# Output products of a Sinkhorn-attention and max-out kernel by Strassen's algorithm, with its sums on three engines and its steps in one list

## The chip, the cores and the metric

One Trainium2 chip, one of its cores. The core has TensorE (PE, with its weight loads shown apart as PEld), VectorE (DVE), ScalarE (ACT), GpSimd (POOL) and SyncE (SP), which run side by side and wait for each other through semaphores; transfers run on 16 DMA engines, fed by SP's queue and POOL's queue. The metric is the device time of one execution in microseconds (us), lower is better. Before: 166.56 us, the median of 3 runs (165.94 to 166.78).

## The reference

There are 4 batches, 8 heads, 768 positions and 64 elements a head. A Sinkhorn-normalised 8x8 matrix per batch and head mixes the 8 blocks (96 positions each) of keys and of values; each block of queries then attends to its own mixed block. The result, 768 tokens of 512 for each batch, goes through a max-out layer.

```python
for _ in range(5):
    P = P - np.max(P, axis=-1, keepdims=True)
    P = np.exp(P)
    P = P / (np.sum(P, axis=-1, keepdims=True) + 1e-09)
    P = P / (np.sum(P, axis=-2, keepdims=True) + 1e-09)
k_sorted = np.einsum('bhij,bhjcd->bhicd', P, k_b).reshape(B, H, S, D)
v_sorted = np.einsum('bhij,bhjcd->bhicd', P, v_b).reshape(B, H, S, D)
...
scores = scale * np.matmul(q_b, k_sb.transpose(0, 1, 2, 4, 3))
...
x = np.ascontiguousarray(attn_out.transpose(0, 2, 1, 3)).reshape(B * S, H * D)
h1 = x @ w1
h2 = x @ w2
g = np.maximum(h1, h2)
return (g @ w_out).astype(np.float32)
```

w1 and w2 are 512x1024, w_out is 1024x512, x has 3072 rows.

## The kernel before, in words

The max-out is rewritten: max(h1, h2) = relu(x(w1 - w2)) + x w2, so the output is relu(x(w1 - w2)) w_out + x (w2 w_out). The kernel forms w1 - w2 once (`w_difference`, two quarters of it on POOL), transposes w2 on TensorE and forms w2 w_out once into `wc` (`w_product`, line 657). The output of a batch is then one product with 12 blocks of 128 in its inner dimension: 8 blocks of g (`g_tiles`) against `wo_sb` and 4 blocks of x transposed (`xT`) against `wc`. All matmul operands are bf16, sums are fp32.

A batch passes these steps, each of which takes one PSUM tile (two banks; there are four such tiles) and frees it when an engine has read it: `sort_k` (line 458, three per batch) mixes the keys; `sort_v`, `sort_v_pair`, `sort_v_halved` (lines 479, 523, 500) mix the values, from `v_dc`, a turned copy of `v_raw` made in column quarters by `turn_v` (line 250); `q_transposes` (lines 433 and 419) turn the queries, on TensorE in batches 0 and 1 and by a DMA transpose on SP's queue in batches 2 and 3, from `q_pair`, which `pair_q` (line 407) copies together; `scores` (line 548; exp on ACT, line 556, into one of NE buffers e); `values` (line 575; reciprocal and multiplication on DVE, lines 586 and 592); `x_transposes` (line 605), a DMA transpose on SP's queue from batch 1 on, four per batch; `moe_h` (line 677; relu on ACT or DVE), eight per batch, one for each half of the batch's tokens (`ch`) and two 128-blocks of g; and `moe_out` (line 704), which for a tile of 128 tokens runs 12 matmuls of 512 columns. Two tiles share a PSUM tile, which ACT or DVE copies out whole (1024 columns) and SP stores (512 KB). The last two token tiles of batch 3 are done by `moe_out_last` (lines 737 to 740), in one piece of 512 columns and two of 384 and 128, the last one copied and stored by ACT.

xT of one batch has halves by `ch` and, within each, two parts that come from one `x_transposes` each: the parts 0 and 1 belong to ch 0, the parts 2 and 3 to ch 1. A `moe_h` of ch 1 reads part 2 in its first two matmuls and part 3 in the next two.

Loads of k, q, v and weights are issued by POOL (lines 143, 160, 169, 182, 189). Batch 3's keys and queries are loaded into `v_raw`, once `turn_v` has emptied it: `load_k(3)` into its first half of columns, `load_q(3)` into the second.

The order on each engine is the order of the program's text (manual schedule). After a hand-written front for batch 0, four loops over `units` (line 848 on) run the h and output units of a batch, and tables (`first_tail`, `second_tail`, `third_tail`) say which attention steps of the next batch follow which unit. `pick` gives each PSUM read to ACT or DVE by running loads.

Of the kernel before, what the change touches and what calls it, by code (L numbers as in the profile page):

```python
# [10 lines left out]
FP32 = mybir.dt.float32  # L11
BF16 = mybir.dt.bfloat16
# [4 lines left out]
def kernel(  # L17
# [24 lines left out]
    G = B * H  # L42
# [10 lines left out]
    NE = 8  # L53
# [188 lines left out]
    def turn_v(rows, eng, c0, c1):  # L242
# [6 lines left out]
        else:  # L249
            nc.vector.tensor_copy(  # L250
# [152 lines left out]
    def pair_q(b, two):  # L403

        if two == 0:
            q_pair[b] = qpool.tile([128, HP, R, 2 * D], BF16, tag="q_pair", name="q_pair", bufs=1)
        nc.vector.tensor_copy(
            out=q_pair[b][:, :, :, two * D : (two + 1) * D],
            in_=q_raw[b][:, two * HP : (two + 1) * HP].rearrange("p h (r d) -> p h r d", r=R),
        )  # L410
        load["D"] += 900
# [125 lines left out]
    e_tiles, x_tiles = {}, {}  # L537

    def scores(b, u, n=0):
# [15 lines left out]
        e = e_bufs[(b * 8 + u) % NE]  # L555
# [98 lines left out]
    def w_product(dmt):  # L654
        ps = ps_f32("wc_ps")
        for fb in range(NFB):
            nc.tensor.matmul(  # L657
                ps[:, 0:512],
                w2T[:, fb, dmt * 128 : (dmt + 1) * 128],
                wo_sb[:, fb, :],  # L660
                start=(fb == 0),
                stop=(fb == NFB - 1),
            )
        evac(wc[:, dmt, :], ps[:, 0:512], 512)
# [33 lines left out]
    out_ps = {}  # L698

    def out_products(dst, b, ti, n0=0, n1=512, part=None):  # L700
        ch, off = divmod(ti * 128, TCH)
        for m in range(NFB + HP) if part is None else range(part * 6, part * 6 + 6):
            hp = m - NFB
            nc.tensor.matmul(  # L704
                dst,
                g_tiles[b, ch, m // 2][:, m % 2, off : off + 128]
                if m < NFB
                else xT[:, b % 2, ch, hp % 2, hp // 2, off : off + 128],
                wo_sb[:, m, n0:n1] if m < NFB else wc[:, hp, n0:n1],
                start=(m == 0),  # L710
                stop=(m == NFB + HP - 1),
            )

    def moe_out(b, ti, part):
        slot = ti % 2
        if slot == 0 and part == 0:
            out_ps[0] = ps_f32("out_ps")
        ps = out_ps[0]
        out_products(ps[:, slot * 512 : (slot + 1) * 512], b, ti, part=part)
        if slot == 1 and part == 1:  # L720
            tok0 = b * S + ti * 128
            o = opool.tile([128, 2, 512], FP32, tag="o", name="o")
            evac(o.rearrange("p t n -> p (t n)"), ps, 1024)
            nc.sync.dma_start(
                out=out[tok0 - 128 : tok0 + 128, :].rearrange("(t p) n -> p t n", p=128),
                in_=o,
            )

    def moe_out_last(ti, pieces):

        tok0 = (B - 1) * S + ti * 128
        for n0, n1, eng in pieces:
            ps = ps_f32("out_ps")
            out_products(ps[:, 0 : n1 - n0], B - 1, ti, n0, n1)
            o = opool.tile([128, n1 - n0], FP32, tag=f"o{ti}{n0}", name="o", bufs=1)
            if eng == "A":
                nc.scalar.copy(out=o, in_=ps[:, 0 : n1 - n0])
            else:
                nc.vector.tensor_copy(out=o, in_=ps[:, 0 : n1 - n0])  # L739
            (nc.scalar if eng == "A" else nc.sync).dma_start(  # L740
                out=out[tok0 : tok0 + 128, n0:n1], in_=o
            )


    def att(b):

        SC = [lambda u=u: scores(b, u) for u in range(8)]
        VA = [lambda u=u: values(b, u) for u in range(8)]
        TR = [lambda t=t: x_transposes(b, t) for t in range(4)]
        return SC, VA, TR  # L750
# [96 lines left out]
    def turn(rows, c0):  # L847
        turn_v(rows, "D", c0, c0 + 24)
        load["D"] += 850

    def sorts_and_scores(b):
        SC, VA, TR = att(b)
        return SC, VA, TR, [lambda t=t: sort_k(b, t) for t in range(3)]

    SC, VA, TR, KS = sorts_and_scores(1)
    VS = [lambda t=t: sort_v_pair(2, t) for t in range(8)]
    TQ = [lambda half=half: q_transposes(1, half) for half in range(2)]
    TURN = [lambda c=c: turn(both, c) for c in (0, 24, 48, 72)]
    first_tail = {
        7: KS,  # L860
        9: [TQ[0], TURN[0]],
        10: [SC[0], TQ[1], TURN[1]],
        11: SC[1:4] + TURN[2:4] + [lambda half=half: load_v(3, half=half) for half in range(2)],
        12: VS[0:3],
        13: VS[3:6],
        14: VS[6:8] + [SC[4]],
        15: [VA[0], lambda: pair_q(2, 0)],
        16: [VA[1], lambda: pair_q(2, 1)],
        17: SC[5:8] + [TR[0]],
        18: [VA[2]],  # L870
        19: [VA[3], TR[1]],
        20: [VA[4]],
        21: [VA[5], TR[2]],
        22: [VA[6], VA[7], TR[3]],
    }
    SC, VA, TR, KS = sorts_and_scores(2)
    VS = [lambda t=t: sort_v_halved(3, t) for t in range(4)]
# [90 lines left out]
```

## Time and profile before

| | us |
|---|---|
| median of the runs | 166.56 |
| span of the profiled execution, first to last instruction | 165.0 |
| TensorE busy (2007 matmuls) | 157.0 |
| DVE, ACT, POOL busy | 77.5, 82.3, 33.9 |
| output matmuls of 512 columns, line 704, 261 recorded | 67.5 busy |
| h matmuls of 384 columns, line 677, 256 | 44.5 busy |
| copies of 1024 output columns, ACT, 10 | 10.1 |

Busy time of a matmul is its whole duration in the pipeline, which overlaps the next one's (379 ns recorded for 512 columns, though they follow each other every 217 ns): the pace is read from the chain of work or from start times. A few matmul records can be missing. By stages, TensorE is busy 31.88 of the 32.70 us from 38.40 to 71.10 (batch 0's output with batch 1's attention), 32.58 of 33.20, 31.08 of 31.30 and 26.21 of 26.40 in the next three; DVE 18.34, 17.74, 11.30 and 1.25 in the same four. POOL has 3.55, 3.40, 0 and 0 there, all of it loads.

### The profile page before, as it was taken

To read this page: it belongs to the slowest core of one execution; us is meant where nothing else is said; L and a number is where in the kernel's file an instruction comes from. 1 tells how busy PE (TensorE), PEld (TensorE's weight loads), DVE (VectorE), ACT (ScalarE), POOL (GpSimd) and SP (SyncE) were. 2 spreads that over 40 slices of the span, in tenths; PEclk is the share of its full clock that TensorE was granted. 3 is DMA by queue.
4 is the path that set the end of the run, shared out by engine and by line. 5 is a ranking of instruction groups with operands and counts; after the bars stand their busy time and mean duration, and the time that the engine had idled before them with its cause. 6 is when DMAs were issued, how large, how long until landed. Compare 5 with 4: busy or idle time off the path is not lost.

```text
span 165.0 us, 4561 instructions
## 1 busy us (share of the span) xinstructions
PE 157.0 (95%) x2007; PEld 95.4 (58%) x2025; DVE 77.5 (47%) x170; ACT 82.3 (50%) x101; POOL 33.9 (21%) x61
## 2 busy tenths in 40 slices
PE   7889999999999999999999999999999999999992
PEld 7839776756554555557655554575655546654451
DVE  4878995684366564525277763250642420000011
ACT  3489776617239846055652353457447206642020
POOL 7949997131206000000014010000000000000000
PEclk9999999999999999999999999999999999999999
DMA  3999999999999999689515999995025294000333
GB/s 41 204 204 194 164 196 207 209 205 220 210 203 204 220 224 167 175 84 228 111 19 104 126 212 157 200 309 29 0 52 175 50 164 142 0 0 0 127 131 127
DMA packets 30404, 23.90 MB, mean 145 GB/s; under 512 B 16752, under 2 KB 25200, under 8 KB 30384
## 3 DMA queue, kind: packets, MB, share of 16 engines
q0 software_dynamic: 11040, 13.37, 50.0%
q1 hardware_dynamic: 19200, 10.17, 28.9%
q8 instruction: 16, 0.26, 0.7%
q10 hardware_dynamic: 144, 0.07, 0.1%
q14 instruction: 4, 0.03, 0.1%
HBM read 26.75 MB, written 6.29 MB: 200 GB/s over the span
## 4 chain that ended last, share of the span: by engine, by line
PE 81%; DMA 6%; DVE 5%; ACT 3%; POOL 2%; issue 2%
PE out_ps L704 37%; PE h_ps L677 25%; DMA w_sb<-in_moe_w_dram 5%; PE wc_ps L657 4%; PE o_ps L575 4%; PE k_ps L458 3%; PE s_ps L548 3%; ACT e L556 1%; POOL w_sb L189 1%; PE v_ps L523 1%; DMA p_sb<-in_sort_net_dram 1%; PE tq_ps L433 1%; DVE colsum L276 1%; DVE p_sb L273 1%; PE tw_ps L638 1%
## 5 line engine op out<-in xcount | busy, mean ns | idle before, releaser
L704 PE MATMUL out_ps<-wo_sb,g 128*128 128x512 bf16 (+2 forms) x187 | 46.0, 370 | 1.4 <-issue 1.0
L677 PE MATMUL h_ps<-xT,w_sb 128*128 128x384 bf16 x256 | 44.5, 326 | 0.0
L677 PEld LDWEIGHTS <-w_sb 128*128 128x128 bf16 x256 | 24.0, 98 | 15.5
L556 ACT ACTIVATE e<-s_ps 96x768 bf16<-96x768 f32 x32 | 24.0, 805 | 14.8 <-PE s_ps L548 14.8
L691 ACT ACTIVATE g<-h_ps 128x768 bf16<-128x768 f32 x27 | 21.7, 811 | 17.4 <-PE h_ps L677 17.3
L704 PEld LDWEIGHTS <-g 128*128 128x128 bf16 x200 | 17.1, 97 | 15.8
L704 PE MATMUL out_ps<-wc,xT 128*128 128x512 bf16 (+2 forms) x98 | 24.7, 370 | 0.1
L108 ACT COPY o<-out_ps 128x1024 f32<-128x1024 f32 x10 | 10.1, 1012 | 28.0 <-PE out_ps L704 25.2
L592 DVE TENSOR_TENSOR x<-o_ps,rs 96x512 bf16<-96x512 f32 x32 | 22.0, 687 | 1.1
L704 PEld LDWEIGHTS <-xT 128*128 128x128 bf16 x100 | 9.6, 97 | 11.2
L575 PEld LDWEIGHTS <-e 96*128 96x128 bf16 x256 | 11.7, 97 | 5.7 <-DVE v_sb L110 0.2
L586 DVE RECIPROCAL rs<-o_ps 96x8 f32<-96x8 f32 x32 | 6.4, 201 | 17.2 <-PE o_ps L575 17.1
L739 DVE COPY o<-out_ps 128x512 f32<-128x512 f32 (+1 forms) x2 | 1.2, 625 | 27.6 <-PE out_ps L704 27.6
L575 PE MATMUL o_ps<-v_sb,e 96*128 96x65 bf16 x256 | 12.7, 193 | 0.0
L110 DVE CAST kT<-k_ps 128x1024 bf16<-128x1024 f32 x6 | 7.2, 1222 | 8.4 <-PE k_ps L458 8.4
L110 DVE CAST v_sb<-v_ps 96x1024 bf16<-96x1024 f32 x7 | 8.5, 1219 | 4.9 <-PE v_ps L523 2.2
L160 POOL DMA_DIRECT2D v_raw<-in_k_dram x3 | 2.5, 838 | 35.1 <-DVE v_dc L250 31.4
L108 ACT CAST v_sb<-v_ps 96x1024 bf16<-96x1024 f32 x9 | 8.8, 1015 | 1.6 <-PE v_ps L500 0.8
L169 POOL DMA_DIRECT2D v_raw<-in_v_dram x11 | 6.5, 593 | 12.7 <-DVE v_dc L250 6.4
L693 DVE TENSOR_SCALAR g<-h_ps 128x768 bf16<-128x768 f32 x5 | 4.8, 957 | 8.9 <-PE h_ps L677 8.8
L548 PEld LDWEIGHTS <-kT 64*128 64x128 bf16 x256 | 6.1, 94 | 4.8 <-issue 2.6
L548 PE MATMUL s_ps<-qT,kT 64*128 64x96 bf16 x256 | 8.5, 204 | 0.3 <-DVE qT L110 0.2
(97 smaller groups left out, 144.4 us busy)
## 6 DMA issues: line engine op xcount, KB each, us to landing
out_dram<-o SPq DMA_DIRECT2D x11, 512.0 KB, 3.4
v_raw<-in_v_dram POOLq DMA_DIRECT2D x8, 384.0 KB, 13.5
k_raw<-in_k_dram POOLq DMA_DIRECT2D x9, 256.0 KB, 11.0
w_sb<-in_moe_w_dram POOLq DMA_DIRECT2D x4, 256.0 KB, 6.0
w_sb<-in_moe_w_dram POOLq DMA_DIRECT2D x2, 512.0 KB, 9.6
wo_sb<-in_moe_w_out_dram POOLq DMA_DIRECT2D x2, 512.0 KB, 13.7
v_raw<-in_v_dram POOLq DMA_DIRECT2D x3, 256.0 KB, 5.0
q_raw<-in_q_dram POOLq DMA_DIRECT2D x4, 192.0 KB, 9.1
```

The lines of the kernel that those rows point to most:

```text
L108: nc.scalar.copy(out=out_ap, in_=in_ap)
L110: nc.vector.tensor_copy(out=out_ap, in_=in_ap)
L169: nc.gpsimd.dma_start(out=v_raw[r0 : r0 + 64, m * n : (m + 1) * n], in_=v_src[b, :, m * n : (m + 1) * n],)
L548: nc.tensor.matmul(ps[:, h2 * 512 + ii * 128 : h2 * 512 + ii * 128 + BLK], kT[b][rows, (hp * 8 + i) * BLK : (hp * 8 + i) * BLK + 128], rhs ...
L556: nc.scalar.activation(out=e[:, 0 : 8 * BLK].rearrange("p (t c r) -> p t c r", t=8, r=R), in_=ps[0:BLK] .rearrange("p (t f) -> p t f", t=8 ...
L575: nc.tensor.matmul(ps[:, h2 * 512 + ii * 65 : h2 * 512 + (ii + 1) * 65], e[:, (h2 * 4 + ii) * BLK : (h2 * 4 + ii) * BLK + 128], v_sb[:, m0 ...
L586: nc.vector.reciprocal(out=rs, in_=ov[:, :, :, 64])
L592: nc.vector.tensor_tensor(out=x, in0=ov[:, :, :, 0:D], in1=rs.to_broadcast([BLK, 2, 4, D]), op=ALU.mult,)
L657: nc.tensor.matmul(ps[:, 0:512], w2T[:, fb, dmt * 128 : (dmt + 1) * 128], wo_sb[:, fb, :], start=(fb == 0), stop=(fb == NFB - 1),)
L677: nc.tensor.matmul(h_ps[ch, t][:, m * 512 : m * 512 + TCH], w1_sb[:, hp, fb * 128 : (fb + 1) * 128], xT[:, b % 2, ch, hp % 2, hp // 2, :], ...
L691: nc.scalar.activation(out=g, in_=src, func=AF.Relu)
L704: nc.tensor.matmul(dst, g_tiles[b, ch, m // 2][:, m % 2, off : off + 128] if m < NFB else xT[:, b % 2, ch, hp % 2, hp // 2, off : off + 12 ...
```

## The change

The output product of a batch is seen as 2x2 blocks: rows in the two token halves a1x (ch 0) and a2x (ch 1); the inner dimension in halves, 4 blocks of g and 2 of x each; columns in halves of 256. Strassen's algorithm (Winograd's form) takes 7 block products in place of 8, on sums and differences of the blocks:

- of the weights, once: t1 = b12 - b11, t2 = b22 - t1, t3 = b22 - b12, t4 = b21 - t2 (here with the sign that the list of products needs), for the g blocks (1024 elements a partition each) and the x blocks (512 each);
- of the data, for each batch: s1 = a21 + a22, s2 = s1 - a11, s3 = a11 - a21, s4 = a12 - s2, in g for two pairs of blocks and in x once, 768 elements a partition each (12 in all).

A `Group` of a batch computes two token tiles of each half (its token letter is P, 12 matmuls of 256 columns a product) or one (U, 6 matmuls). It has one PSUM tile and 7 steps, 0 to 6, one product each, which alternate between the tile's two banks; products that share a bank accumulate. After each step one engine reads one bank: DVE copies, or adds to what is in SBUF; where ACT is named it copies and POOL adds. Steps 5 and 6 end with the stores of the group's two halves (512 KB each for P, 256 KB for U, by SP). Reads and matmuls of different banks are declared free of each other (`apart`), so that a step waits only for reads of its own bank.

All steps from the end of the front on stand in one list of tokens, which replaces the loops, `pick` and the tables. A token is a letter, numbers and an engine (D DVE, A ACT, P POOL): k sort_k, q q_transposes, s scores, v values, x x_transposes, t a quarter of turn_v, b sort_v of a batch, p pair_q, lv, lk, lq loads for batch 3, w a weight sum (0 for g, 1 for x), c w_product, X a sum of x, G of g, h moe_h. x1.3 is batch 1's transpose of part 3, h1.1.2 is moe_h of batch 1, ch 1, t 2. Turn quarters, q pairs and sums can now run on POOL; e buffers go from 8 to 6; the weight sums t2, t4 and those of x lie in w2T, once it has been used.

```diff
-    NE = 8
+    NE = 6
+    NW = DMODEL // 2
...
-            nc.vector.tensor_copy(
+            (nc.gpsimd if eng == "P" else nc.vector).tensor_copy(
...
-    def pair_q(b, two):
+    def pair_q(b, two, eng):
 
         if two == 0:
-            q_pair[b] = qpool.tile([128, HP, R, 2 * D], BF16, tag="q_pair", name="q_pair", bufs=1)
-        nc.vector.tensor_copy(
-            out=q_pair[b][:, :, :, two * D : (two + 1) * D],
-            in_=q_raw[b][:, two * HP : (two + 1) * HP].rearrange("p h (r d) -> p h r d", r=R),
-        )
-        load["D"] += 900
+            q_pair[b] = qpool.tile([128, HP, R, 2 * D], BF16, tag="q_raw", name="q_pair", bufs=1)
+        out = q_pair[b][:, :, :, two * D : (two + 1) * D]
+        in_ = q_raw[b][:, two * HP : (two + 1) * HP].rearrange("p h (r d) -> p h r d", r=R)
+        if eng == "A":
+            nc.scalar.copy(out=out, in_=in_)
+        else:
+            (nc.gpsimd if eng == "P" else nc.vector).tensor_copy(out=out, in_=in_)
...
-        e = e_bufs[(b * 8 + u) % NE]
+        e = e_bufs[e_next[0] % NE]
+        e_next[0] += 1
...
+    sums_g = big.tile([128, 3, 4, TCH], BF16, tag="sums_g", name="sums_g")
+    sums_x = big.tile([128, 4, 2, TCH], BF16, tag="sums_x", name="sums_x")
+    wt_early = big.tile([128, 2, 4, NW], BF16, tag="wt_early", name="wt_early")
+    w2T_flat = w2T.rearrange("p f d -> p (f d)")
+    wt_late = w2T_flat[:, 0 : 8 * NW].rearrange("p (n k f) -> p n k f", n=2, k=4)
+    wt_c = w2T_flat[:, 8 * NW : 16 * NW].rearrange("p (n k f) -> p n k f", n=4, k=2)
...
+    def weight_sums(c, which, eng):
+
+        b11, b12, b21, b22 = weight_blocks(c)
+        t1, t3 = (wt_c[:, 0], wt_c[:, 2]) if c else (wt_early[:, 0], wt_early[:, 1])
+        t2, t4 = (wt_c[:, 1], wt_c[:, 3]) if c else (wt_late[:, 0], wt_late[:, 1])
+        out, in0, in1 = {
+            1: (t1, b12, b11),
+            2: (t2, b22, t1),
+            3: (t3, b22, b12),
+            4: (t4, b21, t2),
+        }[which]
+        eng.tensor_tensor(out=out, in0=in0, in1=in1, op=ALU.subtract)
...
+    def g_sums(b, t, which, eng):
+
+        a11, a12, a21, a22 = [g_tiles[b, ch, t + 2 * half] for ch in range(2) for half in range(2)]
+        s1, s2, s4 = [sums_g[:, n, t * 2 : t * 2 + 2] for n in range(3)]
+        out, in0, in1, op = {
+            1: (s1, a21, a22, ALU.add),
+            2: (s2, s1, a11, ALU.subtract),
+            3: (a21, a11, a21, ALU.subtract),
+            4: (s4, a12, s2, ALU.subtract),
+        }[which]
+        eng.tensor_tensor(out=out, in0=in0, in1=in1, op=op)
...
+    class Group:
+
+        def __init__(self, b, tiles, x_first=True):
+            self.b, self.tiles, self.w = b, tiles, len(tiles) * NW
+            self.ks = [4, 5, 0, 1, 2, 3] if x_first else [0, 1, 2, 3, 4, 5]
+            self.ps = None
+            self.at = 0
+            self.reads = []
+
+        def apart(self, ins, bank, needs=()):
+
+            for n, read in self.reads:
+                if (
+                    n != bank
+                    and read.ins.engine != ins.ins.engine
+                    and all(read is not x for x in needs)
+                ):
+                    tc.declare_no_dep(ins.ins, read.ins, reason="another bank of PSUM")
+
+        def read(self, ins, bank, needs=()):
+            self.apart(ins, bank, needs)
+            self.reads.append((bank, ins))
+            return ins
+
+        def product(self, bank, lw, rw, new):
+            n = 0
+            last = len(self.ks) * len(self.tiles) - 1
+            for k in self.ks:
+                for p, ti in enumerate(self.tiles):
+                    ins = nc.tensor.matmul(
+                        self.ps[:, bank * 512 + p * NW : bank * 512 + (p + 1) * NW],
+                        left(self.b, lw, k, ti * 128),
+                        right(rw, k),
+                        start=new and n == 0,
+                        stop=n == last,
+                        skip_group_check=True,
+                    )
+                    self.apart(ins, bank)
+                    n += 1
...
+        def add(self, ch, half, n, other, needs, eng, spare=False):
+            if eng == "A":
+                to = self.by_tile(self.a) if spare else self.part(ch, half)
+                ins = self.read(nc.scalar.copy(out=to, in_=self.by_tile(self.bank(n))), n, needs)
+                nc.gpsimd.tensor_tensor(out=self.part(ch, half), in0=to, in1=other, op=ALU.add)
+                return ins
+            ins = nc.vector.tensor_tensor(
+                out=self.part(ch, half), in0=self.by_tile(self.bank(n)), in1=other, op=ALU.add
+            )
+            return self.read(ins, n, needs)
...
+        def step(self, at, eng):
+            a = self.by_tile(self.a) if at else None
+            if at == 0:
+                n = len(self.tiles)
+                self.ps = ps_f32("out_ps")
+                self.a = opool.tile([128, self.w], FP32, tag=f"a{n}", name="a", bufs=1)
+                self.o = [
+                    opool.tile([128, n, DMODEL], FP32, tag=f"o{n}", name="o", bufs=2)
+                    for _ in range(2)
+                ]
+                self.product(0, "a11", "b11", True)
+                self.first = self.copy(self.by_tile(self.a), 0, eng)
+            elif at == 1:
+                self.product(1, 2, 2, True)
+                self.second = self.add(1, 0, 1, a, [self.first], eng)
+            elif at == 2:
+                self.product(0, "a12", "b21", False)
+                self.copy(self.part(0, 0), 0, eng)
+            elif at == 3:
+                self.product(1, 1, 1, False)
+                self.third = self.add(0, 1, 1, a, [self.first], eng)
+            elif at == 4:
+                self.product(0, 3, 3, True)
+                self.fourth = self.add(1, 1, 0, self.part(0, 1), [self.third], eng)
+            elif at == 5:
+                self.product(1, 4, "b22", False)
+                self.fifth = self.add(0, 1, 1, a, [self.first, self.fourth], eng)
+                self.store(0)
             else:
+                self.product(0, "a22", 4, False)
+                self.add(
+                    1, 0, 0, self.part(1, 0), [self.first, self.second, self.fifth], eng, True
+                )
+                self.store(1)
...
+        eng = text[-1] if text[-1].isalpha() else None
+        body = text[:-1] if eng else text
+        kind = body.rstrip("0123456789.")
+        n = [int(x) for x in body[len(kind) :].split(".")]
+        engine = {"P": nc.gpsimd, "D": nc.vector}.get(eng)
...
+            key = kind, n[0]
+            if key not in groups:
+                groups[key] = Group(n[0], (0, 1) if kind == "P" else (2,), n[0] > 0)
+            groups[key].step(n[1], eng)
+
+    groups = {}
+    plan = [
+        """
+        w0.1D k1.0D X0.3P X0.1D k1.2D G0.0.1D k1.1A w0.3D G0.1.1D G0.0.2D G0.1.2D c1D q1.0A
+        X0.2D t1.0P c0A q1.1A t1.1D c2D G0.0.4D G0.1.4D s1.2 s1.1 c3A X0.4D t1.2P s1.3 t1.3D
+        s1.0 lv1 P0.0A w1.1D w0.2D w1.3P w1.2D lv0 b2.3A b2.7D b2.0A P0.1D b2.1D b2.2A G0.1.3D
+        b2.4A P0.2D w0.4P s1.4 b2.6D G0.0.3P w1.4P b2.5A P0.3A v1.0 v1.4 v1.1 P0.4A U0.0D P0.5A
+        s1.5 v1.2 P0.6A v1.3 U0.1D U0.2A v1.5 s1.6 x1.0 s1.7 U0.3D x1.1 k2.1A p2.0P p2.1P t3.0P
+        k2.2D k2.0A x1.2 U0.4D v1.7 U0.5A U0.6D v1.6 h1.0.0A h1.0.2D x1.3 h1.1.2A h1.1.0D X1.1P
+        q2.0 s2.0 X1.2D s2.1 h1.0.3D G1.0.1P v2.0 G1.0.2P h1.1.1A v2.1 G1.0.4D h1.1.3D X1.4P
+        h1.0.1D q2.1 t3.1P G1.0.3P s2.2 X1.3P G1.1.1D G1.1.3P G1.1.2D s2.3 P1.0D v2.2 t3.2P x2.0
+        P1.1A v2.3 s2.4 P1.2D s2.5 s2.6 s2.7 x2.1 t3.3D G1.1.4P P1.3D v2.4 P1.4D v2.5 P1.5D
+        U1.0A v2.7 b3.1D P1.6D lq3 v2.6 x2.3 lk3 U1.1A U1.2D b3.2A x2.2 b3.3D U1.3A U1.4A p3.0A
+        U1.5D b3.0D U1.6D h2.1.3D p3.1A h2.0.2D h2.0.0D k3.0A k3.1D k3.2A h2.1.0A h2.0.1A X2.1P
+        q3.0 X2.2D X2.3D s3.0 q3.1 s3.1 h2.1.2D h2.1.1A v3.0 h2.0.3A G2.1.1D G2.1.2D s3.7
+        G2.1.4D s3.3 G2.0.1P P2.0A s3.2 G2.0.3P s3.4 G2.0.2D G2.0.4D G2.1.3P X2.4P P2.1D v3.3
+        P2.2D v3.1 x3.0 v3.4 v3.2 P2.3A P2.4A s3.5 x3.1 s3.6 P2.5A U2.0D U2.1A v3.7 U2.2D v3.6
+        U2.3A v3.5 P2.6A x3.2 x3.3 U2.4A U2.5D U2.6D h3.0.2A h3.0.0A h3.0.1A X3.1P h3.1.0D X3.3P
+        h3.1.2A G3.0.1D h3.0.3A X3.2P X3.4P h3.1.3A h3.1.1A G3.0.3D G3.0.2D U3.0A P3.0A G3.1.1D
+        G3.1.2D P3.1A G3.1.3D P3.2D G3.1.4D U3.1A U3.2D P3.3D G3.0.4D P3.4D P3.5D P3.6A U3.3D
+        U3.4D U3.5D U3.6D
+        """,
+    ]
+    for part in plan:
+        for text in part.split():
+            token(text)
```

## The prediction

> **What bounds the kernel now.** I read the page's busy shares first, then the chain that ended last in order of time, then the timeline of each queue, then the time that single transfers took to land.
>
> ```profile
> PE 157.0 (95%) x2007; PEld 95.4 (58%) x2025; DVE 77.5 (47%) x170; ACT 82.3 (50%) x101; POOL 33.9 (21%) x61
> ...
> PEclk9999999999999999999999999999999999999999
> DMA  3999999999999999689515999995025294000333
> ```
>
> TensorE is busy 95% of the span at full granted clock. The DMA row matters too: the engines are full early, and again for some 20 us after the middle.
>
> ```profile
> 38.40 1.64 PE k_ps L458 x96
> ...
> 64.94 1.30 PE out_ps L704 x6
> ...
> 135.95 10.40 PE h_ps L677 x64
> ...
> 161.95 0.27 ACT o L737
> ```
>
> From 38.40 us to 161.95 us the chain is almost wholly matmuls, so what the change takes from them comes off the end until something makes TensorE wait. The chain also gives paces (time over count): 384 columns in 162.5 ns, 512 in 216.7 ns, the key sort 17 ns. The timeline of the end has one for 128 columns, each with its own weights:
>
> ```profile
> 161.08 0.61 PE L704 MATMUL out_ps<-wo_sb,g 128*128 128x128 bf16 x8
> ...
> 161.53 0.39 PE L704 MATMUL out_ps<-wc,xT 128*128 128x128 bf16 x4
> ```
>
> Eight start within 0.45 us: 56 ns each. So a new set of weights can be loaded every 56 ns, and a 256-column matmul, on the line between 56 and 216.7 ns, takes 109.5 ns although each has weights of its own.
>
> **Products (gain).** Before: 276 x 216.7 + 12 x 162.5 + 12 x 56 ns = 62.4 us. After: 4 batches x 7 products x 3 token tiles x 6 blocks = 504 matmuls x 109.5 ns = 55.2 us. **-7.2 us**, all on the path.
>
> **Sums (hidden).** 29 sums of 768 elements and 5 of weights go to DVE, 19 and 3 to POOL. Rows by shape:
>
> ```profile
> L231 POOL TENSOR_TENSOR w_sb<-w_sb 128x1024 bf16<-128x1024 bf16 x2 | 4.3, 2146 | 0.4 <-DMA w_sb<-in_moe_w_dram 0.4
> ```
>
> ```profile
> L231 DVE TENSOR_TENSOR w_sb<-w_sb 128x1024 bf16<-128x1024 bf16 x2 | 1.3, 688 | 0.3 <-DMA w_sb<-in_moe_w_dram 0.3
> ```
>
> By size, a 768-element sum is 0.55 us on DVE (between 0.52 and 0.69) and 1.65 us on POOL (1.61 to 2.15); POOL's fp32 add of 512 is 1.1 us (1.07 to 2.15). A turn quarter on POOL has no row: copies of 24 and 128 elements take 195 and 299 ns, so 1 ns an element and 0.95 us (DVE's 0.82 to 2.1). From 38.40 on I add up the list's tokens with unit costs from the paces: k 0.545, c 1.73, q1 0.79, s 0.22, b 0.28, v 0.24, h 1.30, P 1.31, U 0.655 us. The four batches need TensorE 31.4, 29.0, 29.5, 24.2 us; DVE 29.1, 23.9, 18.9, 10.1; ACT 22.3, 13.5, 17.3, 8.2; POOL 22.7, 22.0, 14.3, 9.3. No engine outlasts TensorE, so the work itself costs nothing. DVE is the cover nearest its end: 2.3 us in batch 0. If each of its ten 768-element sums there cost 0.69, DVE would take 30.5, still under. Walking batch 0 slot by slot (four PSUM slots, one held by a group), I find waits of 0.5 us before c2, 0.4 before b2.4 and little else: 1.0 us. POOL's order there (turns, lv, three weight sums) ends with w1.4 at c 20.5 (times c: below), ahead of P0.6 at c 24; p2.0 and p2.1 end by c 27 and q2.0 asks for them at c 33.9; t3.0 behind them may wait for the lv pieces until c 29 (13.5 us from c 15.5), still ahead of U0.5's add at c 31.
>
> **Reads per bank (hidden).** Each step's matmuls wait for the read two steps back, not the last one. P: 0.2 us to the last write's end plus 0.69 us (the 512-element copy at line 739) lies under the next product's 1.31. U: 0.2 + 0.42 under 0.655, level within 0.05 us, paid twice at the very end.
>
> **Slips.** Old unit sums give 121.2 us for 123.5 us of chain, 2.3 us of small waits. Batch 0's 1.0 us, and 1.3 us for the other three, keep that: no difference.
>
> **Transfers moved (cost).** SP's queue is in order, and x transposes stand behind the group's stores. I count from 38.40 (time c).
> - x1.3: the list up to v1.6 is 31.45 on TensorE; its normalisation ends and SP issues at c 32.6. Transposes land 2.8 to 5.3 us after issue where no k or q load is due; 3.5 is the one issued right behind a store. So c 36.1. But only two h tiles (2.6 us, where before there were four) and two matmuls come before its reader in h1.1.2: c 34.4. **+1.7** (1.1 to 3.6).
> - q2.0 follows on SP 1.22 us later and lands after 4.4 to 5.2 us, c 38.3 to 39.1, against s2.0 at 38.35: **+0.3** (0 to 0.7).
> - x2.3 and x2.2. This is the large one. The rows of before:
>
> ```profile
> 84.30 0.58 POOL L160 DMA_DIRECT2D v_raw<-in_k_dram  x1 [31.39 <-DVE v_dc L250]
> ...
> 88.59 1.92 POOL L160 DMA_DIRECT2D v_raw<-in_k_dram  x2 [3.71 <-DVE rs L586]
> ...
> 94.62 0.89 POOL L143 DMA_DIRECT2D v_raw<-in_q_dram  x1 [4.11 <-DVE rs L586]
> ```
>
> ```profile
> 99.32 0.38 SPq L724 DMA_DIRECT2D out_dram<-o  x1
> 99.80 1.64 SPq L605 DMA_TRANSPOSE xT<-x  x1
> ```
>
> ```profile
> L605 SPq DMA_TRANSPOSE xT<-x x1: 1638/1638/1638, 99.8 to 99.8; - x1
> DMA to landing us min/median/max: 8.5/8.5/8.5
> ```
>
> While k and q of batch 3 load, transposes issued at 89.2, 95.2 and 99.8 take 7.6, 9.5 and 8.5 us to land, against 2.9 for one issued at 86.7. Before, those loads have 105 us minus 84 to spread over. Now all four pieces follow the last turns, and three turns' quarters and the sums around them are POOL's: from g of h1.1.0 (c 39.45) POOL has in its order seven sums, two turns and a 512 add, 7 x 1.65 + 2 x 0.95 + 1.1 = 14.55 us, with no gap. So lq3 issues at c 54.0 and lk3 behind it until 57, while P1's two 512 KB stores go out at 55.5 and 58.3. x2.3 issues at c 59.25 (list 57.25 plus the 2.0 of waits above), 5.25 us after q, like 99.80 against 94.62; x2.2, 1.2 us later, c 60.45. The first matmul after U1.6, c 62.4, is h2.1.3, which reads x2.2. With 7.6 us it lands at 68.05: **+5.6** (0.85 with 2.8, 7.55 with 9.5). I take the middle of the three, since 8.5 is nearest in place but its store was nearer. Queued behind: h2's eight tiles, key sort 3, all batch 3. p3.0 and p3.1 stand on ACT until q lands (10.5 us, c 64.5), then 3.0 us and a 5 us transpose give q3.0 by 72.5, under the same wait (s3.0: 70.5 + 5.6).
> - x3.3, behind P2's last store (A copy, POOL add, two stores: c 90.2 before waits): lands 94.9, read at 94.15. **+0.8** (0 to 2.5).
>
> **The end (cost).** Before, 64 KB is the last store. Now P3.6's copy and POOL add put 512 KB at 2.0 us after its matmuls, 0.6 us before U3's two 256 KB. Rows land 512 KB in 2.8 and 256 KB in 2.0. Alone, U3's last is 0.5 us later than before; behind the other, 1.7. **+1.1**.
>
> **Sum.** -7.2 + 1.7 + 0.3 + 5.6 + 0.8 + 1.1 = +2.3 on the profiled 165.0 us span: 167.3. The median of the runs is 1.56 us above that span: **168.9 us**.
>
> The Trainium skill speaks against the change in two places. "TensorE: Matmul & The Clock Gate", part 1, says that an idle window of about 3.4 us halves the clock until another has been busy. No slice of before shows a lower clock, nor so long an idle after 38 us; by the page the 5.6 us wait would cost an estimated 1.7 us more, 170.6. "SBUF — State Buffer", section "Who interferes with whom", says that a DVE instruction with two SBUF inputs contends with a GpSimd instruction that reads SBUF. POOL's 2146 ns row ran beside normalisations and copies, none with two such tensor inputs, so no row shows it; if POOL stood still for the DVE sums and turn in lq3's stretch, an estimated 3.0 us, the sum would be 171.9.
>
> **Rivals.** (1) The loads are out of the way: faster. If x2.2 lands after 3.8 us, the median of all twelve, its wait is 1.85 and the time 165.2; with x1.3 and x3.3 at 2.8 us, q2.0 free and the short end it is -7.2 + 1.1 + 0.85 + 0.5 = -4.75: 161.8. Centre 163.5. For it: x issued 2.4 us after the k load at 84.30 still took 2.9. Against: the other three. It decides where lq3 or x2.2 comes 3 us better than I count. (2) POOL becomes the bound: at 2.15 us a sum its seven take 3.5 us longer, lq3 slips to 57.5, and the loads end later by as much: 172.4. For it: POOL's stretch before lq3 has no gap; against: 2.15 is for 1024 elements. (3) The small matmuls don't keep 109.5 ns because weights lie on the path: 97 ns of PEld a matmul in place of 56 would cost nothing below 109, so even a loss of 10 ns each, 5.0 us, is far-fetched against the 56 ns row: 173.9.
>
> **How the numbers follow.** Forecast 0.50, its own range 166.5 to 171.5 (small terms at their ends, x2.2 from 3.5 to 7.5): slower 0.43, same 0.07. Rival 1 0.37: faster 0.33, same 0.04. Rival 2 0.11 and rival 3 0.02, slower, of which 0.01 same. A measurement here tells 0.5%, 0.83 us, from no change. Together faster 0.33, same 0.12, slower 0.55. The range reaches down through rival 1 to 162.0 and up to rival 2, 172.5.
>
> **What would show it.** Out products' pace of 109 to 110 ns; a TensorE gap over 3 us ahead of h2.1.3 released by the transpose of x2; lq3 issued on POOL near 94 us of the span; waits of 1 to 2 us at h1.1.2; POOL without gaps between. The forecast is wrong if x2.2 lands within 4 us, if POOL reaches lq3 before 90 us, or if the pace at 256 columns is above 115 ns.

## The result and the profile after

| | before | after |
|---|---|---|
| median of the runs, us | 166.31 (165.94 to 166.78, 4 runs) | 192.94 (192.53 to 193.5, 4 runs) |
| profiled execution, its span, us | 166.56, 165.0 | 192.64, 190.8 |
| mean granted TensorE clock | 1.00 | 0.949 |

The ratio is 1.159 (95% interval 1.155 to 1.164): the change makes the kernel 16% slower. The forecast was 168.9 us with a range up to 172.5, so the sign was right and the size far off.

First the page of the changed kernel, busy time and the row of the granted clock:

```profile
PE 160.2 (84%) x2226; PEld 118.1 (62%) x2229; DVE 128.3 (67%) x227; ACT 83.7 (44%) x111; POOL 100.8 (53%) x109
...
PEclk9999999999699699999999999669996999999997
```

DVE went from 77.5 to 128.3 us and POOL from 33.9 to 100.8, yet neither is full over the span, and TensorE is at 84%. The clock, full in every slice before, dips in four places before the end. What TensorE waited for, in total, times and longest:

```profile
PE h_ps L680 <- DMA xT<-x: 10.0, 6, 6.9
PE out_ps L804 <- DVE sums_g L750: 5.1, 2, 3.3
PE out_ps L804 <- DVE w2T L726: 3.7, 1, 3.7
PE wc_ps L660 <- DVE wc L111: 3.1, 1, 3.1
```

The first line is the transposes, which were foreseen. The three others, 11.9 us, are waits for VectorE, which were not. The chain that ended last (start, us, engine, what) shows where they sit:

```profile
54.59 6.43 DVE w2T L726
...
82.88 4.14 DMA xT<-x
...
94.20 1.98 DVE sums_g L750
...
116.29 7.75 DMA xT<-x
124.08 5.57 PE h_ps L680 x24
```

A weight sum of 512 elements takes 6.43 us on VectorE, a g sum of 768 takes 1.98; undisturbed they take 0.42 and 0.55 (all_on_dve, below). The last line is the clock: 24 h matmuls, 3.9 us at the pace of before, took 5.57 right after TensorE had stood for 6.9. The groups of VectorE by shape (busy us, mean ns) show that it is no single accident:

```profile
L750 DVE TENSOR_TENSOR sums_g<-sums_g,g 128x768 bf16<-128x768 bf16 x7 | 9.1, 1317 | 0.1
L750 DVE TENSOR_TENSOR sums_g<-g,sums_g 128x768 bf16<-128x768 bf16 x7 | 6.5, 934 | 0.2
...
L726 DVE TENSOR_TENSOR w2T<-wc,w2T 128x512 bf16<-128x512 bf16 x1 | 6.4, 6430 | 0.0
...
L738 DVE TENSOR_TENSOR sums_x<-sums_x,xT 128x768 bf16<-128x768 bf16 x3 | 1.6, 547 | 0.0
```

The same instruction with the same shape takes 547 ns in one group and 1317 in another, without idle time ahead of it: its duration depends on what else runs. GpSimd's timeline across the 6.43 us names it:

```profile
54.28 0.53 POOL L170 DMA_DIRECT2D v_raw<-in_v_dram  x1 [2.77 <-DVE w2T L726]
54.83 1.17 POOL L726 TENSOR_TENSOR w2T<-wc 128x512 bf16<-128x512 bf16 x1
55.93 1.06 POOL L170 DMA_DIRECT2D v_raw<-in_v_dram  x2
57.01 2.14 POOL L726 TENSOR_TENSOR w2T<-wo_sb,w2T 128x1024 bf16<-128x1024 bf16 x1
59.09 1.64 POOL L750 TENSOR_TENSOR g<-g 128x768 bf16<-128x768 bf16 x1
61.16 1.15 POOL L726 TENSOR_TENSOR w2T<-wc,w2T 128x512 bf16<-128x512 bf16 x1 [0.44 <-DVE w2T L726]
```

GpSimd ran the first five lines without a gap, and VectorE's one instruction ended (61.02) 0.3 us after they had (60.73): when GpSimd's next sum had to wait for VectorE's result (the bracket gives the idle time and what ended it). VectorE was not short of data: of its two operands one is its own sum of 53.65, and the other, `wc`, is read by GpSimd's sum at 54.83.

### The profile page after: what moved, and what is told of

It is laid out like the page before. It is cut to its first block, busy times and chain, and to the rows that moved or that the text cites. A ratio compares the mean times of both kernels' runs of the same rounds, so it can differ in the third digit from the quotient of the medians.

```text
span 190.8 us, 5145 instructions
## 1 busy us (share of the span) xinstructions
PE 160.2 (84%) x2226; PEld 118.1 (62%) x2229; DVE 128.3 (67%) x227; ACT 83.7 (44%) x111; POOL 100.8 (53%) x109
## 4 chain that ended last, share of the span: by engine, by line
PE 55%; DVE 21%; DMA 13%; issue 3%; POOL 3%; ACT 1%; SPq 0%; DVEq 0%; POOLq 0%
PE out_ps L804 27%; PE h_ps L680 17%; DMA xT<-x 8%; DVE sums_g L750 8%; DMA w_sb<-in_moe_w_dram 4%; DVE w2T L726 4%; PE o_ps L578 3%; PE k_ps L460 2%; POOL sums_g L750 2%; PE s_ps L550 2%; PE wc_ps L660 2%; DVE wt_early L726 1%; POOL w_sb L190 1%; DVE kT L111 1%; DMA p_sb<-in_sort_net_dram 1%
## 5 line engine op out<-in xcount | busy, mean ns | idle before, releaser
L680 PE MATMUL h_ps<-xT,w_sb 128*128 128x384 bf16 x256 | 46.6, 333 | 10.1 <-DMA xT<-x 10.0
L696 DVE TENSOR_SCALAR g<-h_ps 128x768 bf16<-128x768 f32 x12 | 11.4, 955 | 23.5 <-PE h_ps L680 23.4
L828 POOL TENSOR_TENSOR o<-o,a 128x512 f32<-128x512 f32 (+1 forms) x12 | 11.9, 994 | 24.3 <-ACT o L827 24.3
L738 POOL TENSOR_TENSOR sums_x<-xT 128x768 bf16<-128x768 bf16 x6 | 10.1, 1691 | 17.5 <-DMA xT<-x 17.5
L804 PEld LDWEIGHTS <-sums_g 128*128 128x128 bf16 x144 | 13.9, 100 | 7.6 <-DVE sums_g L750 5.6
L827 ACT COPY o<-out_ps 128x512 f32<-128x512 f32 (+1 forms) x16 | 7.7, 479 | 23.9 <-PE out_ps L804 22.3
L804 PE MATMUL out_ps<-w2T,sums_x 128*128 128x256 bf16 x72 | 11.8, 273 | 3.7 <-DVE w2T L726 3.7
L804 PE MATMUL out_ps<-wo_sb,g 128*128 128x256 bf16 x96 | 14.0, 285 | 0.0
L109 ACT CAST kT<-k_ps 128x1024 bf16<-128x1024 f32 x7 | 7.1, 1012 | 12.8 <-PE k_ps L460 12.8
L804 PE MATMUL out_ps<-w2T,sums_g 128*128 128x256 bf16 x48 | 7.6, 297 | 5.1 <-DVE sums_g L750 5.1
L804 PEld LDWEIGHTS <-sums_x 128*128 128x128 bf16 x96 | 8.6, 98 | 5.2 <-issue 3.9
L660 PE MATMUL wc_ps<-wo_sb,w2T 128*128 128x512 bf16 x30 | 8.7, 430 | 3.2 <-DVE wc L111 3.1
```

Of the source, the lines that this page charges most:

```text
L660: nc.tensor.matmul(ps[:, 0:512], w2T[:, fb, dmt * 128 : (dmt + 1) * 128], wo_sb[:, fb, :], start=(fb == 0), stop=(fb == NFB - 1),)
L680: nc.tensor.matmul(h_ps[ch, t][:, m * 512 : m * 512 + TCH], w1_sb[:, hp, fb * 128 : (fb + 1) * 128], xT[:, b % 2, ch, hp % 2, hp // 2, :], ...
L696: nc.vector.tensor_scalar(out=g, in0=src, scalar1=0.0, scalar2=None, op0=ALU.max)
L738: eng.tensor_tensor(out=out, in0=in0, in1=in1, op=op)
L804: ins = nc.tensor.matmul(self.ps[:, bank * 512 + p * NW : bank * 512 + (p + 1) * NW], left(self.b, lw, k, ti * 128), right(rw, k), start=n ...
L828: nc.gpsimd.tensor_tensor(out=self.part(ch, half), in0=to, in1=other, op=ALU.add)
```

## The experiments

Two readings of the 23.5 us by which the forecast's span of 167.3 was missed: VectorE and GpSimd stand in each other's way when both add in SBUF; or the list simply asks too much of single engines, or lays the late transposes badly, and the long sums only fill time in which VectorE would have waited.

### The price by itself (probe)

In the kernel before, spare sums after three h units of batch 3 (n is 0, 4 or 7), into `w2T` (`scr`), which is no longer read then. VectorE has room there.

```diff
+        for _ in range(2):
+            if n < 7:
+                nc.gpsimd.tensor_tensor(
+                    out=scr[:, 0:768], in0=g, in1=x[:, 0:768], op=ALU.add
+                )
+            else:
+                nc.gpsimd.tensor_copy(out=scr[:, 0:768], in_=g)
+        for _ in range(2):
+            if n != 4:
+                nc.vector.tensor_tensor(
+                    out=scr[:, 768:1536], in0=g, in1=x[:, 768:1536], op=ALU.add
+                )
+            else:
+                nc.vector.tensor_copy(out=scr[:, 768:1536], in_=g)
```

> The kernel before, with six DVE and six POOL instructions added on spare memory in batch 3, where both engines have little to do; output unchanged. They start in pairs at the same event: POOL sums of 768 beside DVE sums of 768, POOL sums beside DVE copies, POOL copies beside DVE sums. Theory 1 (an instruction of DVE that needs a second port of the memory waits until the POOL instruction in flight ends, and POOL's next one may go first): at least one of each pair of DVE instructions takes 1.5 to 3.5 us in place of 0.55 or less, with its end within 0.6 us after the end of a POOL instruction. Theory 2 (POOL's work does not slow DVE; the long DVE sums of the changed kernel wait for operands): all DVE instructions take 0.6 us or less. The span stays at 165 to 166 us in both.

166.03 us (the kernel before, run beside it: 166.26). VectorE's timeline, then GpSimd's, each group two instructions:

```profile
137.40 2.47 DVE L930 TENSOR_TENSOR w2T<-g,xT 128x768 bf16<-128x768 bf16 x2 [5.17 <-ACT g L691]
142.60 2.07 DVE L934 COPY w2T<-g 128x768 bf16<-128x768 bf16 x2 [2.73 <-ACT g L691]
146.50 1.65 DVE L930 TENSOR_TENSOR w2T<-g,xT 128x768 bf16<-128x768 bf16 x2 [1.83 <-ACT g L691]
```

```profile
137.45 3.91 POOL L923 TENSOR_TENSOR w2T<-g,xT 128x768 bf16<-128x768 bf16 x2 [42.72 <-ACT g L691]
142.71 3.46 POOL L923 TENSOR_TENSOR w2T<-g,xT 128x768 bf16<-128x768 bf16 x2 [1.35 <-ACT g L691]
146.60 2.24 POOL L927 COPY w2T<-g 128x768 bf16<-128x768 bf16 x2 [0.43 <-ACT g L691]
```

In the first pair VectorE's first sum took 0.56 us and its second 1.88, ending 0.4 us after GpSimd's first; GpSimd's took 2.00 and 1.9 where one alone takes 1.64. The second line shows that a bf16 copy within SBUF on VectorE waits too (0.36 and 1.68 us), the third that VectorE's sums also wait, though less, beside GpSimd's copies (1.65 us for two, where two alone take about 1.0). So Theory 1's size, 1.5 us or more for one of each pair, came in the first two pairs and not in the third. The conflict is there without the change.

### Its share of the loss (no_dve_sums, no_pool_sums, all_on_dve)

Two kernels leave one engine's sums out; the third computes everything, with all that GpSimd had been given on VectorE.

```diff
 no_dve_sums
-        w0.1D k1.0D X0.3P X0.1D k1.2D G0.0.1D k1.1A w0.3D ...
+        k1.0D X0.3P k1.2D k1.1A ...
 no_pool_sums
-        w0.1D k1.0D X0.3P X0.1D ...
+        w0.1D k1.0D X0.1D ...
 all_on_dve (each X, G, w, t, p on P)
-        w0.1D k1.0D X0.3P X0.1D ... t1.0P ... w1.3P ... p2.0P p2.1P t3.0P ...
+        w0.1D k1.0D X0.3D X0.1D ... t1.0D ... w1.3D ... p2.0D p2.1D t3.0D ...
```

> The changed kernel without the 34 sums that DVE does (29 of data, 5 of weights; the places they would fill hold zeros or old sums, set by POOL once); POOL's sums, turns and loads stay in their order, and so do all transposes. Theory 1 (ports): the DVE time that went into blocked sums is gone, TensorE waits for DVE no more; 168 us, 166 to 173, which is what was forecast with only the transposes' waits. Theory 2 (late loads and transposes are the main loss, as forecast): POOL's list and the loads behind it are as before, so the waits stay; 182 us or more.

> The changed kernel without the 22 sums that POOL does (places as above); POOL keeps turns, pairs, the adds of ACT's copies and the loads, which come earlier. Theory 1: nearly as fast as without DVE's sums, less what turns and adds still block; 163 to 168 us, and DVE sums near 0.55 us each except beside turns and adds. Theory 2: loads for batch 3 issue about 12 us earlier against the products, so the waits before h of batch 2 go but those at h1.1.2 and x3 stay; 175 to 185 us.

> The changed kernel with every sum, turn quarter and query pair that POOL did moved to DVE (full computation). DVE gets about 17 us more of work, 6 us of it in batch 0, where the list leaves it 2 us. Theory 1: blocked time (22 us on DVE) goes, except beside the adds; 172 us, 168 to 177, DVE the bound of batches 0 and 1. If the split among engines was worth its price: 193 us or more.

177.66, 177.30 and 177.45 us. Whichever side is taken away, 15.0 to 15.3 us go, and doing *all* the work on one engine is as good as leaving half of it out. So it is the meeting of the two and not the amount. Nor is it GpSimd's DMA issues: in no_pool_sums the weight sum of the 6.43 us takes 0.41 beside three of them. In all_on_dve VectorE's longest kind of 768-sum averages 553 ns. All the same, the three times lie 5 to 14 us above what Theory 1 gave (168, 163 to 168, 172), because the waits for transposes are 11.1, 9.3 and 8.6 us. no_pool_sums has the time of its Theory 2, but not its mechanism: the wait before h of batch 2 did not go (6.1 us), and TensorE waits for no sum there. TensorE's waits in all_on_dve:

```profile
PE h_ps L680 <- DMA xT<-x: 8.6, 4, 6.0
PE out_ps L804 <- DVE sums_g L750: 1.6, 2, 1.5
```

The transposes are left, at close to what was forecast for them (1.7 + 5.6 + 0.8 = 8.1 us): 1.79 us ahead of h1.1.2 against 1.7, 6.0 ahead of h2.1.3 against 5.6.

### The transposes (h_order, early_loads, both_orders)

All three stand on all_on_dve. h_order issues x1.3 right behind v1.6 and x2.2 ahead of x2.3, and runs the h tiles of half 0 before those that read the late parts. early_loads turns v of batch 3 earlier, on ACT, so that lq3 and lk3 leave sooner.

```diff
 h_order
-        U0.6D v1.6 h1.0.0A h1.0.2D x1.3 h1.1.2A h1.1.0D ... h1.0.3D ... h1.0.1D
+        U0.6D v1.6 x1.3 h1.0.0A h1.0.2D h1.0.3D h1.0.1D h1.1.2A h1.1.0D
-        lq3 v2.6 x2.3 lk3 U1.1A U1.2D b3.2A x2.2 ... h2.1.3D p3.1A h2.0.2D h2.0.0D
+        lq3 v2.6 x2.2 x2.3 lk3 U1.1A U1.2D b3.2A ... p3.1A h2.0.2D h2.0.0D h2.0.1A h2.0.3A h2.1.3D
 early_loads
-        t3.0D k2.2D k2.0A x1.2 ... h1.0.0A ... h1.1.2A ... t3.1D ... t3.2D ... t3.3D ... lq3 ... lk3
+        t3.0A k2.2D k2.0A t3.1A x1.2 ... h1.0.0A t3.2A ... h1.1.2A t3.3A lq3 lk3
```

> The variant with all sums on DVE, with the loads where they were, but h tiles of token half 0 before those of half 1 in batches 1 to 3, x2.2 issued ahead of x2.3 and x1.3 right after its values. Full computation. Theory 1: each wait for a transpose is covered by 2 x 1.3 us more of products (1.3 in batch 3): x1.3 1.8 to 0, x2 by 3.8, x3 by 1.3; 171.5 us, 169 to 174. If waits move to the sums that now come later (G of batch 1 and 2): 175 us or more.

> The variant with all sums on DVE (177.45 us, one look), with batch 3's four turn quarters on ACT and 50 to 15 tokens earlier, and the loads of q and k of batch 3 right behind them, before any transpose of batch 2. Full computation. Theory 1 (transposes share the DMA engines with those loads, as forecast): x2's transposes land in 3 to 4 us in place of 8, TensorE's wait before h of batch 2 falls from 6 to about 1 to 2 us and the clock stays up there; 170.5 us, 169 to 173. Theory 2 (the wait there comes from SP's order, stores first, not from the loads): landing stays near 8 us, 175 us or more.

> Both edits together. Theory 1: no wait for a transpose over 1 us; what stays is DVE in batch 0, about 6 us: 168 us, 166 to 170. If the two edits save the same wait only once: as the better of the two.

170.83, 173.95 and 167.81 us (the kernel before, run beside them: 167.12, and 166.26 beside all_on_dve, each once, so the differences are good to about 1 us). Both edits do what the transposes' mechanism says: from 177.45 the tile order takes 6.6, the loads 3.5, together 9.6. h_order and both_orders come within 1 us of what their Theory 1 gave; early_loads is 1 us slower than its Theory 1 allowed: the transposes of 93.8 to 105.0 us land after 3.1 to 4.5 us, as it said, but TensorE still waits 2.4 us for one. With the loads gone, the three transposes of 91.7 to 102.7 us in both_orders land 3.7 to 4.6 us after issue; in all_on_dve those that share the engines with the loads take 7.8 and 8.8. In both_orders TensorE waits 0.7 us for transposes and its clock is 1.00.

### Sharing without meeting (balanced)

From both_orders, ACT gets two turn quarters and some reads, GpSimd a few sums and q pairs at places where VectorE only reads PSUM.

```diff
-        c1D ... t1.0D ... q1.1A ... t1.2D ... G0.1.3D b2.4A P0.2D w0.4D ... G0.0.3D w1.4D ... p2.0D p2.1D
+        c1A ... t1.0A ... q1.1D ... t1.2A ... w1.2D lv0 G0.1.3P G0.0.3P w0.4P w1.4P ... p2.0P p2.1P
```

> Both edits, and in batch 0 DVE relieved: two more turn quarters, two copies of wc and h tiles and one of v go to ACT; four late sums (G0.0.3, G0.1.3, w0.4, w1.4) and the q pairs go back to POOL, placed where DVE's list holds reads of PSUM only. Full computation. Theory 1 (what blocks is only the pair POOL with a DVE instruction of two operands in SBUF or a copy within it): these POOL instructions cost nothing, DVE's 35 us in batch 0 fall to 30; 164 us, 162 to 167, near or under the kernel before. If any POOL work slows DVE: DVE's reads of PSUM stretch and it is no better than both orders alone.

167.87 us. GpSimd's sums beside VectorE's PSUM reads cost those nothing (its v casts 1.21 us and normalisations 0.69, as ever), so the placing works. But nothing comes of it: VectorE's work from 38.4 to 100 us fell from 51.2 to 44.9 us, yet batch 1's first h matmul starts at 72.6 us against 72.1, and the chain that ended last now holds one of ACT's new turn quarters (1.57 us at 49.30), ahead of an exp of ACT. Against the 164 us of Theory 1 it is a miss.

### Order alone, with the sums shared (order_only, h_order_shared)

Both lay the order edits into the changed kernel as it is, VectorE and GpSimd sharing the sums: order_only those of both_orders, h_order_shared only those of h_order.

```diff
 order_only against both_orders
-        ... X0.3D ... t1.0D ... w1.3D ... X1.1D ... G1.0.1D ... X2.1D ...
+        ... X0.3P ... t1.0P ... w1.3P ... X1.1P ... G1.0.1P ... X2.1P ...
```

> The order of both_orders (early loads, tiles of half 0 ahead of the late transposes) with the changed kernel's own sharing of the sums between VectorE and GpSimd (the eighth, t3.0 to t3.3, stays on ScalarE, as there). Theory of two separate causes that add up: the order is worth 9.6 us where VectorE holds every sum (177.4 to 167.8), so here 192.6 - 9.6 = 183, with VectorE's 768-sums still 0.9 to 2 us each in the trace. Rival 1 (the order was the cause, and slow sums only filled its idle time): 168 to 171. Rival 2 (the slow sums set the pace, so the order is worth little while they last): 189 to 193.

> Only the order of the tiles and of the two transposes, as in h_order, laid into the changed kernel, whose sums stay shared between VectorE and GpSimd and whose loads stay where they were. In order_only the trace shows why its 189.4 us is not a clean answer: the early load of the last q stood on GpSimd's queue from 82 to 89.9 us for ScalarE's turn of the last v_raw, and the x and g sums of batch 1 stood behind it. Without that load the order alone is measured. With every sum on VectorE it was worth 6.6 us (177.45 to 170.83). Two causes that add: 192.6 - 6.6 = 186.0, with the stretched sums left as they are (768-sums of VectorE 0.9 to 1.3 us on average). Rival, the slow sums hold the pace after the late transposes anyway: 189 to 192.5.

189.36 and 185.75 us. order_only isn't clean. GpSimd's timeline (the bracket is idle time and its releaser):

```profile
81.28 0.72 POOL L828 TENSOR_TENSOR o<-o,a 128x256 f32<-128x256 f32 x1 [3.90 <-ACT o L827]
89.94 0.93 POOL L144 DMA_DIRECT2D v_raw<-in_q_dram  x1 [7.93 <-ACT v_dc L246]
...
92.47 1.67 POOL L738 TENSOR_TENSOR sums_x<-xT 128x768 bf16<-128x768 bf16 x1
```

The early load waits for ACT's turn, and the sums of batch 1 stand behind it on the same queue. order_only's time is that of its rival 2. h_order_shared hits the additive number (186.0), but for a wrong reason. Up to batch 1's first h matmul its list is the changed kernel's but for x1.3, which SP issues; still that matmul starts at 77.63 us against 81.62. VectorE's timeline at the place of the 6.43 us, in h_order_shared:

```profile
54.48 0.42 DVE L726 TENSOR_TENSOR w2T<-wc,w2T 128x512 bf16<-128x512 bf16 x1
```

and GpSimd's:

```profile
53.99 0.53 POOL L170 DMA_DIRECT2D v_raw<-in_v_dram  x1 [2.70 <-DVE w2T L726]
54.54 1.38 POOL L726 TENSOR_TENSOR w2T<-wc 128x512 bf16<-128x512 bf16 x1
```

Here VectorE's sum ran at once, and GpSimd's was stretched a little (1.38 for 1.17). The profile's marks don't say which engine had the memory first: VectorE's start is the earlier one in both kernels, by 0.06 us here and by 0.24 in after (54.59 against 54.83), where it had to wait all the same. What they show is that a shift of 0.2 us between the two engines turned 0.42 us into 6.43. 4.0 of the 6.9 us are this luck, at which no edit aimed, and the order's own worth is 2.9 us where the sums are shared, against 6.6 where they aren't. So the two causes overlap: rival 2 of order_only's expectation is the nearer one. From after to h_order_shared TensorE's waits for transposes fall from 10.0 to 2.9 us, and those for g sums rise from 5.1 to 6.5: while VectorE's sums are stretched, a transpose that comes sooner finds the sums not ready.

### What the version is worth once both are mended (best, best_2)

best is both_orders with sums of product 2 ahead of those of products 4 and 5, x1.3 earlier, one read given to ACT and P3.6 to VectorE. best_2 moves the sums of products 4 and 5 further back, and v1.7 and v1.6 forward.

```diff
 best against both_orders (batch 2; batch 1 alike)
-        G2.1.4D s3.3 G2.0.1D P2.0A s3.2 G2.0.3D s3.4 G2.0.2D G2.0.4D G2.1.3D X2.4D P2.1D v3.3 P2.2D
+        G2.0.1D G2.0.2D s3.3 P2.0A s3.2 s3.4 P2.1D v3.3 X2.3D G2.0.3D G2.1.3D G2.0.4D G2.1.4D X2.4D P2.2D
 best_2 against best
-        v3.3 X2.3D G2.0.3D G2.1.3D G2.0.4D G2.1.4D X2.4D P2.2D ... P2.3A P2.4A
+        v3.3 P2.2D ... X2.3D G2.0.3D G2.1.3D P2.3A G2.0.4D G2.1.4D X2.4D P2.4A
```

> The run with both orders and every sum on VectorE, with the last waits of its trace taken by order alone. In its trace TensorE still waited 2.1 us for sums_g at L750 (89.38 and 122.18 us), 1.2 us for e of L559 (82.10 us), 0.7 us for the transposes (72.10 us). Here the sums that product 2 of batches 1 and 2 reads are laid ahead of those that products 4 and 5 read, v1.6 and x1.3 ahead of the single tile's last steps, h1.1.1 between s2.1 and v2.0, h1.1.3 is read by ScalarE, and P3.6 is read by VectorE instead of ScalarE and GpSimd, so that the last stores do not stand behind a GpSimd addition. Theory (what is left of the forecast's 7.2 us of products is eaten only by these waits): 167.8 - 2.1 - 1.2 - 0.7 - about 0.8 at the end = 163.0, faster than before by some 3 us, TensorE's idle time after 38 us under 1.5 us. Rival (VectorE as such is the bound now, 117.7 us of work against its reads, so the waits come back a few steps later): 166.5 to 168, with new waits for sums or for g at L694 and L696 of the same 4 us.

> As best, with its own last wait taken by order: in best's trace TensorE waited 1.5 us at 125.84 us and 0.4 us at 94.20 us for VectorE's reads L837 and L830, which stood behind six sums laid ahead of them, and 0.5 us at 69.70 us for v1.6 behind kT. The sums that product 4 reads are laid behind the read of product 2 and those that product 5 reads behind the read of product 3. Theory: 165.7 - 1.5 - 0.4 - 0.3 = 163.5, some 2.7 us under before. Rival (VectorE has no room left in these stretches, the wait goes over to the sums again): 165 to 166.

best: 165.73 us (165.35 to 165.95, 8 runs), before 166.23; ratio 0.9966 (0.9953 to 0.9979). It is ahead of the kernel before by a third of a per cent only, between the 163.0 us of its theory and the 166.5 to 168 of its rival. best_2: 170.04 us (169.22 to 171.93, 6 runs), ratio 1.023 (1.018 to 1.029), slower than both its theory and its rival. TensorE's timeline of best, then of best_2:

```profile
125.84 0.60 PE L804 MATMUL out_ps<-w2T,sums_x 128*128 128x256 bf16 x4 [1.48 <-DVE o L837]
```

```profile
95.97 0.61 PE L804 MATMUL out_ps<-wc,sums_x 128*128 128x256 bf16 x4 [1.29 <-DVE sums_x L738]
...
128.79 0.61 PE L804 MATMUL out_ps<-w2T,sums_x 128*128 128x256 bf16 x4 [2.65 <-DVE sums_x L738]
```

In best six sums delay a PSUM read, in best_2 the sums come too late for their product: the wait went over, as its rival said, and grew. VectorE has little room in these stretches (busy 6.66 of the 8 us from 118 in best, 6.23 of the 7 from 122 in best_2), though its share of the span is 71%.

## Why the prediction was wrong, step by step

The table cuts each span at batch 1's first h matmul, where batch 0's output ends (times from TensorE's timelines, us):

| | sums | order | first h of batch 1 | from there to the end | span |
|---|---|---|---|---|---|
| before | none | - | 70.9 | 94.1 | 165.0 |
| after | shared | own | 81.6 | 109.2 | 190.8 |
| h_order_shared | shared | tiles | 77.6 | 106.1 | 183.7 |
| all_on_dve | VectorE | own | 71.5 | 104.1 | 175.6 |
| h_order | VectorE | tiles | 72.4 | 96.4 | 168.8 |
| both_orders | VectorE | tiles and loads | 72.1 | 93.6 | 165.7 |
| best | VectorE | both and sums | 72.4 | 91.7 | 164.1 |

**Sums (hidden): the step that failed.** "No engine outlasts TensorE, so the work itself costs nothing" set each engine's load against TensorE's as if the engines were independent. They are not: 15.2 us of the span go when VectorE and GpSimd no longer add side by side, 10.1 of them in batch 0, where the forecast found 1.0 us of waits. The forecast wrote the cause down, from the Trainium skill's "SBUF — State Buffer", section "Who interferes with whom": a VectorE instruction with two SBUF inputs contends with a GpSimd instruction that reads SBUF. But it left it out of the sum and priced it at 3.0 us, as GpSimd standing still for VectorE's time in one stretch. The traces show the other direction as the dear one, VectorE waiting through GpSimd's 1.6 to 2.1 us and once through several in a row. The prices of single sums held: 0.55 and 1.65 us forecast for 768 elements, 0.55 and 1.64 measured alone. But their rows are of sums that never met one of the other engine, as the forecast says itself ("so no row shows it"), and what no row shows went into the sum as nothing.

The 15.2 us leave 8.3 of the 23.5. all_on_dve shows where they went, about: 3.2 to output products that gained less than forecast, 2.1 to waits beyond those forecast for transposes, 2.4 to other matmuls, which ran in part at half the clock (0.51 from 110.4 to 117.3 us), and 0.7 to the end (the first three from start to start on TensorE's timeline from 38 us on, against before).

**GpSimd's prices.** A turn quarter on GpSimd was put at 0.95 us and takes 1.5 to 1.9; the 512 add 1.27 against 1.1. Beside VectorE's sums its 768-sum takes up to 2.26 us against 1.65. lq3 left GpSimd at 107.78 us, where 94 had been expected; 10.8 us of that is batch 0's lateness.

**Transfers moved.** Right in mechanism and near in size. The gap ahead of h2.1.3, over 3 us and released by x2's transpose, came: 6.92 us, forecast 5.6. x2.2 landed after 7.7 us (7.6 forecast), but left only 0.9 us before TensorE was ready for it, not 1.95. x1.3 was 1.7 forecast, 1.65 measured after and 1.79 in all_on_dve; x3.3 0.8 and 0.82; q2.0 cost nothing (0.3). The clock's loss, which the forecast gave in a sentence aside and left out of the sum, was real: 24 h matmuls in 5.57 instead of 3.9 us, 1.7 us. Behind the 3.7 us wait at 61 us came another, 12 products in 2.65 us instead of 1.31. The granted clock was 0.50 from 62.3 to 65.7 us and 0.51 from 120.3 to 127.2. The skill's page on the clock gate ("TensorE: Matmul & The Clock Gate", part 1) puts half the clock behind an idle window of about 3.4 us, until another has been busy. The lengths agree, 3.4 us here and 6.9 there. In these runs less was enough, though not always: half the clock also came with waits of 3.1 us (after, 48.6 to 52.1) and 3.3 us (144.2 to 147.7), and in no_pool_sums with one of 1.6 us (79.0 to 82.4, 0.51), while best_2's wait of 2.65 us had none.

**Products.** The pace was right: 126 products in 13.86 us on the chain's last stretch, 110 ns, forecast 109.5. The gain was not all there. Start to start on TensorE's timeline, without waits of over 0.15 us, the output products from 38 us on take 61.1 us before and 56.8 in best: 4.3, not 7.2. Of the missing 2.9 us 1.3 are on the side of before, whose 62.4 held some 1.0 us of small waits; 1.6 are on the other side, mostly in the groups that follow attention steps, where 12 matmuls take 1.42 us on the chain in place of 1.31.

**Reads per bank, Slips, the end.** No output product of after waits over 0.15 us for a read of its bank, as forecast; in best such waits come (1.5 us the longest), because VectorE does other work first. "No difference" for slips falls with the sums. The end was +1.1 forecast, between 0.5 alone and 1.7 behind the other store: from TensorE's last matmul on, before takes 3.05 us and after 4.82, +1.8. With P3.6 taken off GpSimd, in best, it is 3.96, +0.9.

**Rivals.** None of them. Rival 2 came nearest in naming GpSimd, but it made GpSimd the bound by its own work; GpSimd is at 53% and it is VectorE that it holds up. Rival 3 is ruled out by the pace.

Why almost nothing was left in the end: of best's 4.3 us of products, 2.5 go to new waits (3.4 against 1.0 before, from 38 us on) and 0.9 to the end; the other matmuls take 61.6 us in both. 0.9 is left of the span. Whether a better list could win those waits back stays open; best_2 shows that moving these sums further back does not.

## What to carry to other kernels

Before adding engines' loads up, ask which of them can't run at the same time: in these runs two-input sums and copies within SBUF on VectorE, and sums and copies on GpSimd beside them, behaved as one resource, and the slower partner set the price. Give GpSimd its work where VectorE reads PSUM, or leave it all on VectorE. And where a transfer comes late, look first at what could run in front of its reader: a change of tile order was worth more (6.6 us) than sooner loads (3.5 us).

## What the runs showed of the hardware that was not expected

- A VectorE sum of 512 elements, 0.41 us alone, lasted 6.43 us (6.44 in order_only) across GpSimd's DMA issues and three sums: it did not get in between them. In the probe VectorE's second sum did get in behind one GpSimd sum; why it did not here stays open.
- A shift of 0.2 us between two engines decided whether that wait came, and by it 4.0 us of the whole: one kernel's profile is not the price of an overlap.
- A one-input bf16 copy in SBUF on VectorE also waits (1018 ns mean beside GpSimd's sums); VectorE instructions with one input in PSUM do not (0.69 us beside GpSimd's work).
